# Spectral filter rows: 14 of 32 GpSimd gathers replaced by plain strided copies on the sync queue

## Chip, cores and metric

One core of one Trainium2 chip. The metric is the device time of one launch in microseconds (us), the median over executions. "Before" is the tuned kernel, "after" the changed one.

## The reference, cut to what matters

```python
x = A_x                                          # [1, 2048, 640] bf16
xn = _layernorm(x)
X = rfft2(xn, axes=(-2, -1))                     # 2048 x 321 complex
s = irfft2(X * (A_w_r + 1j * A_w_i))             # filter: 2048 x 321, two bf16 arrays
g = silu((gelu(xn @ B_w_gate) * (xn @ B_w_up)) @ B_w_down)
return x + s * g
```

A spectral branch (a two-dimensional transform, a filter, the inverse) and a feed-forward branch (three large matrix products) are computed side by side. The change touches only how the rows of the filter reach on-chip memory.

## The kernel before: the parts that matter

The transform along the sequence is done as matrix products. Its frequencies come in eight groups G of 128 rows. For each group the filter is needed twice: at the frequencies k (`pm = 0`, "positive") and at the mirrored ones 2048 - k (`pm = 1`), real and imaginary part each. A row is 321 values, 642 bytes. All four pieces were fetched by indirect gathers on GpSimd (POOL), with the row numbers in a table `LANE`:

```python
WF = [persist.tile([P, 2, 2, LP], BF16, name=f"WF{i}") for i in range(3)]   # three filter buffers
# ...
def gather(G):
    sw = Slot("W")

    def go(e):
        sw.tile = WF[G % 3]
        if 0 < G < 3:      # a 1x1 copy that reads BU: holds groups 1 and 2 back until BU has landed
            nc.gpsimd.tensor_copy(out=gate, in_=sB.tile[0:1, 8 * G - 8, 0:1])
        for pm in range(2):
            for ri, wsrc in enumerate((A_w_r, A_w_i)):
                nc.gpsimd.indirect_dma_start(
                    out=sw.tile[:, pm, ri, 0:L], out_offset=None, in_=wsrc,
                    in_offset=bass.IndirectOffsetOnAxis(ap=LANE[:, 2 * G + pm:2 * G + pm + 1], axis=0))
    W_in[G] = add(go, "POOL", (4200, 4200), (3, G), ...)      # estimated cost in ns, rank
# ... the only two readers, on VectorE:
def m1(e):    # L651
    nc.vector.tensor_tensor(out=sM.tile, in0=sw.tile, in1=sV.tile, op=ALU.mult)
def m3(e):    # L659, after it WF[G % 3] may be filled for group G + 3
    nc.vector.tensor_tensor(out=sN.tile, in0=sw.tile, in1=sV.tile[:, :, ::-1, :], op=ALU.mult)
```

The kernel does not issue its work in the order of the text. Each piece is a task with an estimated cost and a rank, and a small planner in Python lays the tasks out in time; what each engine executes, and in which order, follows from that plan. An engine works its list in order. Semaphore waits are added from the data that an instruction reads and writes.

Names in the profiles: `WF` filter rows, `BU` the regrouped transform input in on-chip memory, `zt`, `Z`, `ma`, `mc` pieces of the spectral branch on VectorE (DVE) and ScalarE (ACT), `pg`, `pu` feed-forward products in PSUM, `ge`, `uT` what ACT and DVE make of them, `sp` PSUM of the spectral branch.

Of the kernel before, what the change touches and what calls it, by code (L numbers as in the profile page):

```python
# [16 lines left out]
P = 128  # L17
S = 2048
D = 640
L = 321  # L20
# [113 lines left out]
class Plan:  # L134
# [11 lines left out]
    def add(self, emit, eng, cost, rank, after=(), new=(), use=(), size=0, slow=1.0, hold=0):  # L146
        engs = eng if isinstance(eng, dict) else {eng: cost}
        t = Task(emit=emit, engs=engs, rank=rank, after=list(after), new=list(new), size=size, slow=slow, hold=hold, seq=len(self.tasks))
        for s in (*new, *use):
            s.users.append(t)  # L150
        self.tasks.append(t)
        return t
# [70 lines left out]
def c_dve(n, rate=2, psum=False, extra=0):  # L223
    d = ((120 if psum else 58) + n / rate) / 0.96 + extra
    return d + 10, d + 130
# [3 lines left out]
def kernel(  # L229
# [11 lines left out]
    nc = tc.nc  # L241
# [22 lines left out]
    gate = consts.tile([1, 1], BF16)  # L264
# [9 lines left out]
    WF = [persist.tile([P, 2, 2, LP], BF16, name=f"WF{i}") for i in range(3)]  # L274
# [12 lines left out]
    add = plan.add  # L287
# [15 lines left out]
    def dma(out, in_, rank, size, after=(), new=(), use=(), slow=1.0, eng=None):  # L303
        return add(lambda e: nc.sync.dma_start(out=out() if callable(out) else out, in_=in_() if callable(in_) else in_),  # L304
                   "SP", (430, 430), rank, after=after, new=new, use=use, size=size, slow=slow)
# [54 lines left out]
    def keep_warm(n, after, src=None):  # L360
        def go(e):
            if heat.tile is None:
                place(heat, (2, 512))
            for k in range(n):
                nc.tensor.matmul(heat.tile[:, k % 2, :], lhsT=idle.tile[:, 0:P], rhs=idle.tile if src is None else X[:, src, 0:512],
                                 start=True, stop=True, skip_group_check=True)
        return add(go, "PE", (n * 430, n * 430), (0, -9), after=after, new=[] if heat.users else [heat], use=[idle, sX] + ([heat] if heat.users else []))
    t = add(blank, "DVE", (330, 400), (0, -9), new=[idle])
    t = keep_warm(6, [t])
# [3 lines left out]
    t = keep_warm(4, [t, x_in[0]], 0)  # L373
# [19 lines left out]
    turned, stored, xn_of = {}, {}, {}  # L393

    def stats(n1, engs):
        x = X[:, n1, :]
        mean, var, rstd = MVA[:, n1, 0:1], MVA[:, n1, 1:2], RSTD[:, n1, :]
        junk = Slot("th")

        eng = engs[0]  # L400
        after = [x_in[n1]] + ([aps[3]] if n1 > 3 else [])

        def moments(e):
            for g in range(2):
                nc.vector.bn_stats(out=STAT[:, n1, 6 * g:6 * g + 6], in_=x[:, 320 * g:320 * g + 320])  # L405
            nc.vector.bn_aggr(out=MVA[:, n1, :], in_=STAT[:, n1, :].rearrange("p (g s) -> p g s", g=2))
            nc.vector.tensor_scalar_add(out=var, in0=var, scalar1=1e-5)  # L407

        def total(e):
            nc.scalar.activation(out=place(junk, (D,)), in_=x, func=ACT.Copy, scale=-1.0 / D, accum_out=NM[:, n1, :])  # L410

        def square(e):
            nc.scalar.activation(out=junk.tile, in_=x, func=ACT.Square, scale=1.0, bias=NM[:, n1, :], accum_out=var)
        if eng == "DVE":
            t = add(moments, "DVE", (1200, 1340), (2, n1), after=after, use=[sX])
        else:
            t = add(total, "ACT", (870, 1000), (2, n1), after=after, new=[junk], use=[sX])
            t = add(square, "ACT", (930, 1100), (2, n1), after=[t], use=[junk, sX])

        def root(e):  # L420
            if eng == "ACT":
                nc.gpsimd.tensor_scalar(out=var, in0=var, scalar1=1.0 / D, scalar2=1e-5, op0=ALU.mult, op1=ALU.add)
            nc.gpsimd.tensor_tensor(out=rstd, in0=var, in1=mh, op=ALU.pow)  # L423
        n = 0 if eng == "DVE" else 1
        return add(root, "POOL", (300 * n + 600, 300 * n + 700), (1, n1), after=[t]), eng
# [84 lines left out]
    for n1 in range(NSLAB):  # L510
        if n1 % 2 == 0:
            xn_of[n1 // 2] = Slot("s1")
        r = stats(n1, (lead[n1] if n1 < 4 else ("ACT" if n1 % 2 else "DVE"),))
# [10 lines left out]
    sB = Slot("xb")  # L524
    B_in = {}
# [18 lines left out]
    W_in, W_slot = {}, {}  # L544

    def gather(G):
        sw = Slot("W")

        def go(e):
            sw.tile = WF[G % 3]  # L550
            if 0 < G < 3:
                nc.gpsimd.tensor_copy(out=gate, in_=sB.tile[0:1, 8 * G - 8, 0:1])
            for pm in range(2):
                for ri, wsrc in enumerate((A_w_r, A_w_i)):
                    nc.gpsimd.indirect_dma_start(  # L555
                        out=sw.tile[:, pm, ri, 0:L], out_offset=None, in_=wsrc,
                        in_offset=bass.IndirectOffsetOnAxis(ap=LANE[:, 2 * G + pm:2 * G + pm + 1], axis=0))
        W_in[G] = add(go, "POOL", (4200, 4200), (3, G), use=[sB] if 0 < G < 3 else [], after=[stored[7]] + ([W_in[G - 1], B_in[2 * G - 2]] if 0 < G < 3 else [W_in[G - 1]] if G else []), new=[sw],
                      size=328704, slow=1.3)
        W_slot[G] = sw  # L560
    for G in range(8):
        gather(G)
    for k in ("t2", "fm", "ft"):
# [7 lines left out]
    def spectral(G):  # L571
# [39 lines left out]
        for ri in range(2):  # L611
# [14 lines left out]
            def cp(e, ri=ri, pe=pe):  # L626
                if ri == 0:
# [4 lines left out]
                    after=[z_done, zt_done, tab_in["fm"], tab_in["ft"]] + firsts)  # L632
            firsts.append(a)
            es.append(add(cp, either(644, act=150), None, (1, 102 + 10 * G), after=[a] + es, use=[pe, sE]))
        sV = Slot("mb")
# [9 lines left out]
        rk = (1, 103 + 10 * G)  # L645
        t = add(v1, "DVE", (810 + (480 if G == 0 else 0), 900 + (480 if G == 0 else 0)), rk, after=es, new=[sV], use=[sE])
        sw, sM, sN, sY, sR = W_slot[G], Slot("mc"), Slot("mc"), Slot("Y"), Slot("R")
# [16 lines left out]
        def m5(e, h):  # L664
            if h == 0:
                place(sR, (2, 2, LP))
            R, Y = sR.tile, sY.tile[64 * h:64 * h + 64]
            Yf = Y.rearrange("p a b f -> p (a b) f")
            for ri in ((1, 0) if h else (0, 1)):
                o = R[64 * ri:64 * ri + 64, h]  # L670
                if ri:
                    nc.vector.tensor_tensor(out=o, in0=Yf[:, ::-3, :], in1=Yf[:, 1:3, :], op=ALU.subtract)
                else:
                    nc.vector.tensor_tensor(out=o, in0=Y[:, 0], in1=Y[:, 1], op=ALU.add)
            if G == 0 and h == 0:
                nc.vector.tensor_copy(out=R[0:1, 0], in_=Y[0:1, 0])
                nc.vector.tensor_scalar_mul(out=R[64:65, 0, 0, :], in0=Yf[0:1, 3, :], scalar1=-1.0)
                nc.vector.tensor_copy(out=R[64:65, 0, 1, :], in_=Yf[0:1, 2, :])
        t = add(m1, "DVE", c_dve(1288), rk, after=[t, W_in[G]], new=[sM], use=[sw, sV])
        t = add(m2, "DVE", c_dve(644), rk, after=[t], new=[sY], use=[sM])  # L680
        t = add(m3, "DVE", c_dve(1288), rk, after=[t], new=[sN], use=[sw, sV])
        t = add(m4, "DVE", c_dve(644), rk, after=[t], use=[sN, sY])
        sI, ius = Slot("IU"), []
        for h in range(2):
            ex = 750 if G == h == 0 else 0
            t = add(lambda e, h=h: m5(e, h), "DVE", (960 + ex, 1050 + ex), rk, after=[t], new=[] if h else [sR], use=[sY, sR] if h else [sY])
# [15 lines left out]
    for G in range(8):  # L702
        spectral(G)
# [212 lines left out]
```

## Time and profile before

| before | value | where |
|---|---|---|
| time, median of the first three executions | 206.83 us (206.66 to 206.9) | the times |
| span of the profiled execution | 209.8 us | the page |
| PE busy | 199.8 us, 95% | the page, part 1 |
| DVE busy / POOL busy | 161.2 / 55.6 us | the page, part 1 |
| gathers on POOL | 32, 33.2 us together | the page, part 5 |
| longest idle time of PE | 2.5 us, at 72.1 to 74.5 us | the waits of PE |

The page of before. In parts 1 and 5 the columns are busy time, share or mean, and idle time with what ended most of it; the row "POOL" with digits is busy tenths in 40 slices.

```profile
PE 199.8 (95%) x1385; PEld 119.9 (57%) x1385; DVE 161.2 (77%) x340; ACT 106.2 (51%) x185; POOL 55.6 (27%) x83
PE   7899899999999779999999999999999999999992
...
PE 77%; DMA 9%; DVE 6%; SPq 4%; ACT 2%; issue 1%; ACTq 0%; DVEq 0%
...
L555 POOL DMA_INDIRECT WF<-in_A_w_r_dram,LANE x16 | 16.5, 1034 | 25.3 <-DVE mc L659 22.5
L555 POOL DMA_INDIRECT WF<-in_A_w_i_dram,LANE x16 | 16.7, 1044 | 4.9 <-issue 4.9
```

PE is full except at the ends and in one place (the two sevens in the middle). The gathers wait for a free buffer (`mc L659`), and nothing in the chain is a gather. In the view of the tile WF the first reader, L651, has no idle time before it; the gathers themselves are the only ones that wait (us, times):

```profile
L651 DVE TENSOR_TENSOR mc<-WF,mb x8: 809/824/829, 80.9 to 128.2; 128x1288 bf16<-128x1288 bf16 x8
...
who waited for it (us, times):
  POOL WF L555: 22.5, 5
```

The longest waits of PE in before, longest in total first (us in total, times, longest):

```profile
PE sp L619 <- DVE zt L297: 2.5, 1, 2.5
PE sp L365 <- DVE uT L358: 1.2, 1, 1.2
```

The timeline of before around that wait (start, us, engine, line, what, and in brackets the idle time before it with what ended it):

```profile
69.30 0.61 PE L582 MATMUL sp<-T,BU 128*128 128x128 bf16 x8
...
69.44 0.95 POOL L555 DMA_INDIRECT WF<-in_A_w_r_dram,LANE  x1 [0.30 <-issue]
...
70.69 0.95 POOL L555 DMA_INDIRECT WF<-in_A_w_i_dram,LANE  x1 [0.31 <-issue]
70.83 1.24 PE L793 MATMUL pg<-xnT,Wg 128*128 128x512 bf16 x5
73.13 1.08 ACT L805 ACTIVATE ge<-pg 128x512 bf16<-128x512 f32 x2 [3.69 <-PE pg L793]
73.25 1.23 DVE L297 CAST zt<-sp 128x1024 bf16<-128x1024 f32 x1 [2.19 <-PE pg L793]
...
74.53 0.45 PE L619 MATMUL sp<-FT,zt 128*128 128x322 bf16 x2 [2.46 <-DVE zt L297]
```

The product `L582` that the cast `zt` reads was, by its own record, through at 69.91 us. DVE was free from 71.06 us on. Yet the cast began at 73.25, and what ended its wait was a signal of PE. ACT waited 3.69 us for PE in the same place.

### The profile page before, as it was taken

To read this page: it belongs to the slowest core of one execution; us is meant where nothing else is said; L and a number is where in the kernel's file an instruction comes from. 1 tells how busy PE (TensorE), PEld (TensorE's weight loads), DVE (VectorE), ACT (ScalarE), POOL (GpSimd) and SP (SyncE) were. 2 spreads that over 40 slices of the span, in tenths; PEclk is the share of its full clock that TensorE was granted. 3 is DMA by queue.
4 is the path that set the end of the run, shared out by engine and by line. 5 is a ranking of instruction groups with operands and counts; after the bars stand their busy time and mean duration, and the time that the engine had idled before them with its cause. 6 is when DMAs were issued, how large, how long until landed. Compare 5 with 4: busy or idle time off the path is not lost.

```text
span 209.8 us, 3765 instructions
## 1 busy us (share of the span) xinstructions
PE 199.8 (95%) x1385; PEld 119.9 (57%) x1385; DVE 161.2 (77%) x340; ACT 106.2 (51%) x185; POOL 55.6 (27%) x83
## 2 busy tenths in 40 slices
PE   7899899999999779999999999999999999999992
PEld 2574344575545356677765444457775656645771
DVE  3897989996324179999989999992366999994464
ACT  4685962444333147867766434322356758642221
POOL 3513422073027500725755810000000222221100
PEclk9999999999999999999999999999999999999999
DMA  6999999699589500113333251016900444542022
GB/s 196 308 318 323 363 285 254 107 285 168 175 279 351 164 3 0 44 41 108 107 97 112 60 160 62 5 62 177 387 3 0 125 128 125 166 130 82 30 67 63
DMA packets 30947, 31.07 MB, mean 148 GB/s; under 512 B 10417, under 2 KB 27457, under 8 KB 30929
## 3 DMA queue, kind: packets, MB, share of 16 engines
q1 hardware_dynamic: 27696, 24.32, 40.0%
q0 software_dynamic: 2368, 5.30, 9.8%
q10 hardware_dynamic: 864, 1.21, 1.6%
q8 instruction: 11, 0.18, 0.4%
q14 instruction: 8, 0.06, 0.1%
HBM read 20.99 MB, written 7.86 MB: 138 GB/s over the span
## 4 chain that ended last, share of the span: by engine, by line
PE 77%; DMA 9%; DVE 6%; SPq 4%; ACT 2%; issue 1%; ACTq 0%; DVEq 0%
PE pg L793 19%; PE pu L793 19%; PE pu L853 12%; PE pg L853 12%; DMA X<-in_A_x_dram 5%; SPq L304 4%; DMA D<-mc 3%; PE sp L692 2%; PE sp L619 2%; PE sp L623 2%; PE sp L724 2%; PE sp L737 2%; PE sp L734 2%; PE sp L599 2%; DVE uT L809 1%
## 5 line engine op out<-in xcount | busy, mean ns | idle before, releaser
L793 PE MATMUL pu<-xnT,Wu 128*128 128x512 bf16 (+1 forms) x270 | 60.7, 356 | 0.0
L793 PE MATMUL pg<-xnT,Wg 128*128 128x512 bf16 (+1 forms) x270 | 60.7, 356 | 0.0
L805 ACT ACTIVATE ge<-pg 128x512 bf16<-128x512 f32 x48 | 28.4, 596 | 42.0 <-PE pg L793 38.5
L853 PEld LDWEIGHTS <-uT 128*128 128x128 bf16 x396 | 37.7, 98 | 14.2
L809 DVE TENSOR_TENSOR uT<-pu,ge 128x512 bf16<-128x512 f32 x48 | 33.0, 688 | 12.7 <-PE pu L793 6.8
L793 PEld LDWEIGHTS <-Wg 128*128 128x128 bf16 x270 | 24.6, 98 | 23.4
L793 PEld LDWEIGHTS <-Wu 128*128 128x128 bf16 x270 | 24.4, 98 | 22.4
L853 PE MATMUL pg<-Wd,uT 128*128 128x320 bf16 (+2 forms) x204 | 31.7, 293 | 0.0
L853 PE MATMUL pu<-Wd,uT 128*128 128x320 bf16 (+1 forms) x192 | 31.0, 298 | 0.0
L818 POOL DMA_DIRECT2D xr<-in_A_x_dram x16 | 8.7, 547 | 70.5 <-DVE res L841 70.5
L297 ACT CAST ma<-sp 128x644 bf16<-128x644 f32 (+1 forms) x28 | 21.8, 794 | 9.2 <-PE sp L623 4.4
L555 POOL DMA_INDIRECT WF<-in_A_w_r_dram,LANE x16 | 16.5, 1034 | 25.3 <-DVE mc L659 22.5
L862 ACT ACTIVATE th<-pg 128x320 f32<-128x320 f32 (+2 forms) x17 | 7.3, 429 | 21.6 <-PE pg L853 18.2
L555 POOL DMA_INDIRECT WF<-in_A_w_i_dram,LANE x16 | 16.7, 1044 | 4.9 <-issue 4.9
L867 DVE SCALAR_TENSOR_TENSOR G<-th,pg 128x320 bf16<-128x320 f32 (+2 forms) x17 | 8.0, 471 | 11.4 <-ACT th L862 10.5
L423 POOL TENSOR_TENSOR RSTD<-MVA,mh 128x1 f32<-128x1 f32 x16 | 9.9, 618 | 22.2 <-DVE MVA L407 21.6
L867 DVE SCALAR_TENSOR_TENSOR G<-th,pu 128x320 bf16<-128x320 f32 (+1 forms) x16 | 7.7, 482 | 6.9 <-ACT th L862 6.9
L297 ACT CAST Vt<-sp 128x640 bf16<-128x640 f32 x13 | 8.8, 693 | 5.7 <-PE sp L724 5.7
L405 DVE BATCH_NORM_STATS2 STAT<-X 128x6 f32<-128x320 bf16 x18 | 7.9, 482 | 2.7 <-DMA X<-in_A_x_dram 2.7
L297 ACT CAST IU<-sp 128x640 bf16<-128x640 f32 x12 | 8.2, 692 | 3.4 <-PE sp L692 2.8
L862 ACT ACTIVATE th<-pu 128x320 f32<-128x320 f32 (+1 forms) x16 | 7.0, 440 | 5.3 <-PE pu L853 4.8
L619 PE MATMUL sp<-FT,zt 128*128 128x322 bf16 x32 | 7.0, 301 | 2.5 <-DVE zt L297 2.5
(80 smaller groups left out, 248.9 us busy)
## 6 DMA issues: line engine op xcount, KB each, us to landing
BU<-D SPq DMA_DIRECT2D x8, 640.0 KB
D<-mc SPq DMA_DIRECT2D x8, 320.0 KB
D<-IU SPq DMA_DIRECT2D x8, 320.0 KB
xr<-in_A_x_dram POOLq DMA_DIRECT2D x16, 160.0 KB
out_dram<-res SPq DMA_DIRECT2D x15, 160.0 KB
Wg<-in_B_w_gate_dram SPq DMA_DIRECT2D x6, 320.0 KB
Wu<-in_B_w_up_dram SPq DMA_DIRECT2D x6, 320.0 KB
Wd<-in_B_w_down_dram SPq DMA_DIRECT2D x2, 960.0 KB
```

Of the source, the lines that this page charges most:

```text
L297: return nc.scalar.copy(out=out, in_=in_) if e == "ACT" else nc.vector.tensor_copy(out=out, in_=in_)
L304: return add(lambda e: nc.sync.dma_start(out=out() if callable(out) else out, in_=in_() if callable(in_) else in_), "SP", (430, 430), rank ...
L423: nc.gpsimd.tensor_tensor(out=rstd, in0=var, in1=mh, op=ALU.pow)
L555: nc.gpsimd.indirect_dma_start(out=sw.tile[:, pm, ri, 0:L], out_offset=None, in_=wsrc, in_offset=bass.IndirectOffsetOnAxis(ap=LANE[:, 2 * ...
L619: nc.tensor.matmul(pt[:, bank, 0:LP], lhsT=tl, rhs=FT[:, ft, :], start=True, stop=False, skip_group_check=True)
L793: nc.tensor.matmul(ps.tile[:, lo:hi], lhsT=w[:, c, t * P:(t + 1) * P], rhs=xnT[:, c, grp * 512 + lo:grp * 512 + hi], start=(c == 0), stop= ...
L805: nc.scalar.activation(out=ge.tile, in_=pg.tile, func=ACT.Gelu_apprx_tanh)
L809: nc.vector.tensor_tensor(out=u.tile, in0=pu.tile, in1=ge.tile, op=ALU.mult)
L818: nc.gpsimd.dma_start(out=sx.tile, in_=xv[:, n1, :])
L853: nc.tensor.matmul(ps.tile[:, 0:hi - lo], lhsT=uT[grp, t].tile[:, j * P:(j + 1) * P], rhs=Wd[:, t, lo:hi], start=(t == 0), stop=(t == 11))
L862: nc.scalar.activation(out=th.tile[:, 0:hi - lo], in_=ps.tile[:, 0:hi - lo], func=ACT.Tanh, scale=0.5)
L867: nc.vector.scalar_tensor_tensor(out=G2.tile[:, lo:hi], in0=th.tile[:, 0:hi - lo], scalar=1.0, in1=ps.tile[:, 0:hi - lo], op0=ALU.add, op1 ...
```

## The change

Its intent: the positive rows k are regular (16 blocks of 4 neighbouring rows, 128 apart, for each half of the partitions), so no gather is needed for them. For groups 1 to 7 they are copied by four plain strided DMAs of 64 rows on the sync queue (SP), and POOL gathers only the mirrored rows: 18 gathers instead of 32, 28 copies more. Bytes and row length stay the same.

```diff
     def gather(G):
-        sw = Slot("W")
+        sw, got, pms = Slot("W"), [], (1,) if G else (0, 1)
# ... the gate copy moves into go_held; POOL's estimated cost is 2100 ns per pm
-            for pm in range(2):
+            for pm in pms:
                 for ri, wsrc in enumerate((A_w_r, A_w_i)):
                     nc.gpsimd.indirect_dma_start(...)
# ...
+        if G == 0:
+            return
+        for h in range(2):
+            for ri, wsrc in enumerate((A_w_r, A_w_i)):
+                k = 8 * G + 4 * h
+                got.append(dma(lambda h=h, ri=ri: WF[G % 3][64 * h:64 * h + 64, 0, ri, 0:L],
+                               wsrc.rearrange("(k r) f -> k r f", r=P)[:, k:k + 4, :], (0, 1, 100 + G), 41088,
+                               after=got[:1], use=[sw], slow=1.3))
# ... m1 waits for all of W_in[G]
```

More of the change, by code (lines that the diff above doesn't have):

```diff
@@ L546, in gather @@
     def gather(G):
-        sw = Slot("W")
+        sw, got, pms = Slot("W"), [], (1,) if G else (0, 1)
         def go(e):
             sw.tile = WF[G % 3]
-            if 0 < G < 3:
-                nc.gpsimd.tensor_copy(out=gate, in_=sB.tile[0:1, 8 * G - 8, 0:1])
-            for pm in range(2):
+            for pm in pms:
                 for ri, wsrc in enumerate((A_w_r, A_w_i)):
@@ L557, in go, with go_held @@
                         in_offset=bass.IndirectOffsetOnAxis(ap=LANE[:, 2 * G + pm:2 * G + pm + 1], axis=0))
-        W_in[G] = add(go, "POOL", (4200, 4200), (3, G), use=[sB] if 0 < G < 3 else [], after=[stored[7]] + ([W_in[G - 1], B_in[2 * G - 2]] if 0 < G < 3 else [W_in[G - 1]] if G else []), new=[sw],
-                      size=328704, slow=1.3)
-        W_slot[G] = sw
+        held = [B_in[2 * G - 2]] if 0 < G < 3 else []
+        def go_held(e):
+            if held:
+                nc.gpsimd.tensor_copy(out=gate, in_=sB.tile[0:1, 8 * G - 8, 0:1])
+            go(e)
+        cost = 2100 * len(pms)
+        got.append(add(go_held, "POOL", (cost, cost), (3, G), use=[sB] if held else [], after=[stored[7]] + W_in.get(G - 1, [])[:1] + held,
+                       new=[sw], size=164352 * len(pms), slow=1.3))
+        W_in[G], W_slot[G] = got, sw
+        if G == 0:
[6 more added lines that the diff above has]
+                               after=got[:1], use=[sw], slow=1.3))
     for G in range(8):
@@ L678, in m5 @@
                 nc.vector.tensor_copy(out=R[64:65, 0, 1, :], in_=Yf[0:1, 2, :])
-        t = add(m1, "DVE", c_dve(1288), rk, after=[t, W_in[G]], new=[sM], use=[sw, sV])
+        t = add(m1, "DVE", c_dve(1288), rk, after=[t] + W_in[G], new=[sM], use=[sw, sV])
         t = add(m2, "DVE", c_dve(644), rk, after=[t], new=[sY], use=[sM])
```

## The prediction

> **What bounds the kernel now.** The matrix engine. The page's busy table gives PE 199.8 of 209.8 us (95%); the windows view by 10 us gives PE 9.8 to 10.0 of 10 in every window from 80 to 200 us, at a granted clock of 1.00. PE is idle for 10 us in all: about 2 at the start, 4.3 in the last window, and a hole of 2.5 us at 72-74.5 us (waits: "PE sp L619 <- DVE zt"). The chain of waits is 77% PE and 9% DMA (x loads, D2 store), with no filter gather and no POOL in it.
>
> **The part that changes.** 32 gathers (L555, 1.03-1.04 us each, 33 us of POOL's 55.6 busy), four per group, about 1.3 us apart. Nothing waits for them: the tile view of WF shows L651, their first consumer, with no idle time before it in any of its eight runs; the only waits are POOL's own, for a buffer ("POOL WF <- DVE mc L659", 22.5 us) and for BU (12.1). Group 0's end at 49.4 for a multiply at 80.9, those of groups 1 and 2 at 71.6; refills run from 84.5, two groups ahead.
>
> **What the change does.** 14 gathers go (about 14.5 us; POOL busy to about 41). In their place the sync queue issues 28 copies of 64 rows of 642 B. At 0.33-0.45 us an issue (as the other stores on that queue) that is 9-12 us of SP within 57-118 us, where SP now waits up to 31.8 us at a stretch. Bytes and row length stay, so DMA load does. The Trainium skill ("DMA: Bandwidth & Descriptors", Issuing engines are not separate DMA queues) says that all issuers share the same 16 DMA engines and that spreading issues saves only sequencer time; here POOL has that time to spare. DVE gets some more semaphore waits (50 ns or less each at L651): an estimated 1-2 us in all, on an engine 77% busy.
>
> **On the critical path: directly nothing.** Three indirect routes remain.
> 1. The kernel orders its instructions by a plan from estimated costs; shorter POOL tasks and more SP tasks shift spectral against feed-forward work. PE's total stays, its holes may move: plus or minus 1 us.
> 2. The stretch 59-70 us is DMA-saturated (share 0.90-1.19 in 1 us windows) and the 2.5 us hole stands at its end, where ACT, DVE and PE all lag while gathers drain till 73. With half the gathers it may shrink by 0-1.5 us. This trace doesn't show that the gathers cause it.
> 3. SP is in order: a copy waiting for a free WF buffer may hold back a D3 store by about 1 us. Only the last store matters (140.8 us); the copies are done by about 120.
>
> **Prediction.** 206.4 us, 204.6 to 208.0 in 8 of 10. Faster by over 2% (under 202.7): 0.04; within 2%: 0.92; slower by over 2%: 0.04.
>
> **What would show it.** 18 gathers of about 1 us on POOL; 28 WF copies on SP; PE still 199-200 us busy; no wait for WF before L651; the chain still about 77% PE; PE full from 80 to 200 us; a hole of 0 to 3 us near 70-75 us.
>
> **What would make it wrong.** Slower: SP copies blocking a store or load that something waits for, or DVE stalling on late copies until PE runs out of fill work: PE holes after 76 us. Faster by over 2%: more than 4 us of PE's idle 10 would have to go, the middle hole and half of the ends, which the change doesn't touch.

## More of the kernel before

The runs of this study fell on two chips, numbered 8 and 14 in the records; for the first measurement of before and after no chip number is recorded. All runs are of one core.

## The result, and the profile after

| | median us | lowest to highest | executions |
|---|---|---|---|
| before | 206.87 | 206.66 to 207.61 | 4 |
| after | 207.06 | 206.92 to 207.19 | 4 |

The ratio of after to before is 1.0007 (95% interval 0.9987 to 1.0028): the same.

The page of after:

```profile
PE 198.5 (97%) x1385; PEld 120.1 (59%) x1385; DVE 161.0 (78%) x340; ACT 106.6 (52%) x185; POOL 41.8 (20%) x69
PE   7799999999999999999999999999999999999991
...
PE 90%; DMA 4%; SPq 1%; ACT 1%; DVE 1%; issue 0%; ACTq 0%
...
L553 POOL DMA_INDIRECT WF<-in_A_w_r_dram,LANE x9 | 9.8, 1084 | 33.9 <-DVE mc L672 32.9
L553 POOL DMA_INDIRECT WF<-in_A_w_i_dram,LANE x9 | 9.7, 1073 | 2.7 <-issue 2.7
```

18 gathers, POOL at 41.8 us, PE's two sevens in the middle gone. The new copies and their first reader in after (duration of the issue in ns, minimum, median, maximum):

```profile
L304 SPq DMA_DIRECT2D WF<-in_A_w_r_dram x14: 536/563/667, 58.2 to 110.2; - x14
L304 SPq DMA_DIRECT2D WF<-in_A_w_i_dram x14: 536/589/1839, 58.9 to 110.8; - x14
...
L664 DVE TENSOR_TENSOR mc<-WF,mb x8: 810/820/828, 76.8 to 123.2; 128x1288 bf16<-128x1288 bf16 x8
```

The same place in the timeline of after; lines of all engines, in order of time:

```profile
67.83 0.61 PE L595 MATMUL sp<-T,BU 128*128 128x128 bf16 x8
...
69.09 1.21 DVE L297 CAST zt<-sp 128x1024 bf16<-128x1024 f32 x1
69.35 1.24 PE L806 MATMUL pg<-xnT,Wg 128*128 128x512 bf16 x5
...
70.43 0.44 PE L632 MATMUL sp<-FT,zt 128*128 128x322 bf16 x2
70.63 0.60 ACT L818 ACTIVATE ge<-pg 128x512 bf16<-128x512 f32 x1 [1.69 <-PE pg L806]
```

The product that the cast reads ended by its record at 68.44 (67.83 + 0.61), the cast began at 69.09, straight behind the instruction before it, and PE took its result up without a wait. The hole is gone and the profiled span is 4.5 us shorter, 205.3 against 209.8. But the times do not differ. Both can be true only if the profiled execution of before was not like the timed ones. Two facts from the builds narrow the question: the lists of instructions of PE, of DVE and of ACT are the same in both kernels, in the same order; only POOL's and SP's lists differ. So the plan did not move any compute.

The trace also records when each semaphore was raised. PE posts one signal per group of matmuls; put side by side with the recorded ends of the groups, in order, they give this for the execution of before just shown (us; from 51 to 66.2 and again from 75 to 90, signal and recorded end agree within 0.1):

```
recorded end   signal    late
66.23          66.24     0.0
67.31          68.82     1.5     the gathers of groups 1 and 2 run on POOL from 61.8
68.39          70.28     1.9     to 71.6 us, eight in a row; their last DMA packet
69.47          73.10     3.6     starts at 72.98 us
69.69          73.16     3.5
69.91          73.22     3.3     <- the product that the cast zt waits for
70.99          73.29     2.3
72.07          73.36     1.3
```

Five signals arrive within 0.26 us. One group of five matmuls takes 1.08 us, so this work was not done in that time: it had been done, and the signals were held back. Over whole traces some signals are not recorded, so there I matched signals and groups such that the lateness is least, and count those over 0.4 us late; these counts and sizes are lower bounds. In before's trace at least 14 signals of PE are late (three near 50 us, behind group 0's four gathers, those of the table, and five from 97 to 106 us, among the refills), in after's none. No signal of ACT, DVE or POOL is late in either.

### The profile page after: what moved, and what is told of

It reads as the page before. It is cut to its first block, busy times and chain, and to the rows that moved or that the text cites. A ratio compares the mean times of both kernels' runs of the same rounds, so it can differ in the third digit from the quotient of the medians.

```text
span 205.3 us, 3793 instructions
## 1 busy us (share of the span) xinstructions
PE 198.5 (97%) x1385; PEld 120.1 (59%) x1385; DVE 161.0 (78%) x340; ACT 106.6 (52%) x185; POOL 41.8 (20%) x69
## 4 chain that ended last, share of the span: by engine, by line
PE 90%; DMA 4%; SPq 1%; ACT 1%; DVE 1%; issue 0%; ACTq 0%
PE pg L806 24%; PE pu L806 24%; PE pg L866 13%; PE pu L866 12%; DMA X<-in_A_x_dram 4%; PE sp L636 2%; PE sp L737 2%; PE sp L750 2%; PE sp L632 2%; PE sp L705 2%; PE sp L747 2%; PE sp L612 2%; PE sp L498 2%; SPq L304 1%; PE sp L595 0%; ACT th L410 0%
## 5 line engine op out<-in xcount | busy, mean ns | idle before, releaser
L553 POOL DMA_INDIRECT WF<-in_A_w_r_dram,LANE x9 | 9.8, 1084 | 33.9 <-DVE mc L672 32.9
L553 POOL DMA_INDIRECT WF<-in_A_w_i_dram,LANE x9 | 9.7, 1073 | 2.7 <-issue 2.7
L297 ACT CAST mc<-sp 128x640 bf16<-128x640 f32 x11 | 7.2, 692 | 3.3 <-PE sp L499 3.3
```

The source lines that it names most:

```text
L297: return nc.scalar.copy(out=out, in_=in_) if e == "ACT" else nc.vector.tensor_copy(out=out, in_=in_)
L553: nc.gpsimd.indirect_dma_start(out=sw.tile[:, pm, ri, 0:L], out_offset=None, in_=wsrc, in_offset=bass.IndirectOffsetOnAxis(ap=LANE[:, 2 * ...
```

## Experiments

Two theories at the start. **Off the path**: the filter loads are hidden and PE sets the time, so nothing about the loads matters; before's page shows an odd execution. **Two effects cancel**: the gathers cause the hole, and the copies cost as much elsewhere.

### First series, chip 8

**Before, unchanged, and after, unchanged.**

> The kernel before, unchanged, with its own profile: is the 2.5 us PE hole at 72-74.5 us of the first profile, and its span of 209.8 us (3 us longer than the median time), usual or a matter of that one execution? Theory 'off the path' (filter loads hidden, PE sets the time): ratio 1.000 +- 0.003 and a profile span of about 205 us with PE idle about 6-8 us and no hole over 1 us at 70-76 us. Rival 'two effects cancel' (the gathers cause the hole, and the new copies cost as much elsewhere): the hole of 2-3 us is there again and the span stays over 208 us.

> The change again, five rounds, to put a narrow interval on its effect. Off the path: 0.998 to 1.003 of before. Rival: the same total, but a profile in which PE has holes over 1 us after 76 us that before lacks.

Measured on chip 8: before 213.94 us (its repeats as the kernel to compare with: 214.14 median of 11), after 207.91 us. The ratio of after to before is 0.9728 (0.9699 to 0.9757), a gain of 2.7%. Neither theory had allowed for this: on this chip the change is clear of noise, and it is before that is slow, by 7 us against the first measurement.

The longest waits of PE in before on chip 8, the same hole, and a second one at about 103 us:

```profile
PE sp L619 <- DVE zt L297: 2.7, 1, 2.7
...
PE sp L619 <- ACT IU L297: 0.9, 1, 0.9
```

Three windows of 10 us of before and then of after on chip 8 (busy us and instructions of each engine, then PE's granted clock, DMA share, GB/s):

```profile
60.00:70.00 10.00, 9.95 (x65) 5.25 (x64) 3.30 (x4) 3.25 (x5) 6.71 (x9) 1.00 1.04 357
70.00:80.00 10.00, 7.25 (x60) 4.54 (x59) 5.91 (x10) 3.60 (x6) 1.28 (x2) 1.00 0.10 21
80.00:90.00 10.00, 9.95 (x77) 6.06 (x75) 9.57 (x21) 8.24 (x11) 4.00 (x4) 1.00 0.10 25
```

```profile
60.00:70.00 10.00, 9.95 (x65) 5.26 (x64) 3.99 (x6) 3.29 (x5) 4.22 (x6) 1.00 1.05 328
70.00:80.00 10.00, 9.89 (x77) 6.24 (x78) 8.58 (x16) 5.92 (x8) 0.00 (x0) 1.00 0.09 29
80.00:90.00 10.00, 9.95 (x79) 6.42 (x80) 9.53 (x19) 7.36 (x11) 2.17 (x3) 1.00 0.15 34
```

PE loses 2.6 us (9.89 less 7.25) in the middle window of before against after. Before has at least 16 late signals, after 2, both at group 0's four gathers. The spread of before has a second part: over its six executions here, spans of 210.2, 210.8, 212.1, 212.3, 212.8 and 213.3 us go with mean granted clocks of 0.998, 0.997, 0.991, 0.989, 0.988 and 0.984. So in most executions with the larger loss PE's clock is lower for a while (one of the 11 repeats does not fit: 211.9 us at 1.000); runs below show where.

**Before without the refills.** An early return leaves out the gathers of groups 3 to 7 (relative error 0.044). Its output is wrong, which doesn't matter for the time.

```diff
         if 0 < G < 3: ...
+            if G > 2:
+                return
             for pm in range(2):
```

> Before with the 20 gathers of groups 3 to 7 left out, so the multiplies reuse stale filter rows (wrong result on purpose); the instruction orders of PE, DVE and ACT are unchanged. Off the path: 206.9 us, ratio 0.997 to 1.002, although 21 us of POOL work and 1.6 MB of DMA are gone. Rival: gathers cost something by contention, so 1 to 4 us faster (ratio 0.98 to 0.995).

Measured: 212.78 us, ratio 0.9913 (0.9869 to 0.9958). With 20 of 32 gathers gone the kernel is 0.9% faster, so the gathers, or the 1.6 MB that they fetch, do cost something without anyone waiting for their data (clear of 1, not of 2%). The hole at the gathers of groups 1 and 2, which this kernel keeps, is still there, and the granted clock in the window from 70 to 80 us is 0.83. The longest wait of PE:

```profile
PE sp L621 <- DVE zt L297: 3.1, 1, 3.1
```

**Before with two more gathers per group** into a tile that nobody reads.

```diff
+    WX = persist.tile([P, 2, 2, LP], BF16, name="WX")
# ... in go, behind the four gathers
+            for ri, wsrc in enumerate((A_w_r, A_w_i)):
+                nc.gpsimd.indirect_dma_start(out=WX[:, 1, ri, 0:L], ..., in_offset=... LANE[:, 2 * G + 1 ...])
```

> Before with two more gathers per group into a tile that nobody reads (48 instead of 32), behind the real ones. POOL per group goes from 5 to about 7.8 us against a group spacing of about 7 us. Off the path: ratio 0.998 to 1.004, L651 still without a wait for WF. Rival: 1 to 3 us slower by contention alone.

Measured: 231.99 us, ratio 1.0851 (1.0804 to 1.0898). Off the path expected at most 1.004, the rival at most 3 us. Both fell. The longest wait of PE in this run, and its windows:

```profile
PE sp L625 <- DVE zt L298: 8.3, 1, 8.3
```

```profile
60.00:70.00 10.00, 9.95 (x65) 5.28 (x65) 3.30 (x4) 2.96 (x5) 6.89 (x9) 1.00 1.05 353
70.00:80.00 10.00, 1.70 (x9) 0.62 (x8) 2.02 (x3) 1.20 (x2) 4.91 (x6) 0.85 0.22 55
80.00:90.00 10.00, 9.78 (x67) 6.25 (x69) 6.74 (x14) 4.72 (x6) 0.00 (x0) 0.81 0.01 2
```

From 70 to 80 us PE, DVE and ACT all but stand still while POOL gathers, with DMA nearly idle (share 0.22): bandwidth is not what is short. The wait of PE for `zt` is 8.3 us here. The granted clock falls to 0.81 to 0.85, so after the hole PE also runs slower for some us: that is a second part of the loss. At least 28 signals of PE are late.

From this came a third theory, **bursts of gathers**: three or more gathers in a row on POOL hold back PE's signals; the change helps because it turns runs of four into runs of two, and the run of eight at 60 to 72 us into two pairs with a pause. Its rival now, **filter latency**: the rows simply arrive sooner.

### Second series, chip 8

Before took 213.79 us (212.12 to 215.32, 7 executions) in this series.

**After with two unread gathers more** per group 1 to 7 (the edit as above, `if G`), so that four stand in a row again.

> New theory 'bursts of gathers': a run of three or more gathers in a row on POOL makes the matrix engine's completion signals arrive late (in the first kernel's trace up to 3.4 us late at 69-72 us), and ACT, DVE and then PE wait for them. This kernel is the change with two more gathers per group (1 to 7) into a tile that nobody reads, so that each group issues four in a row again, while the sync copies stay. Bursts: the gain is lost, time like before on the same chip (ratio 0.99 to 1.01), PE hole of 2 us or more at 66-76 us, late PE signals in the trace. Rival 'filter latency' (the change wins because rows are there sooner): still like the change, ratio about 0.973 where before takes 214 us.

Measured: 214.81 us, ratio 1.0053 (0.9965 to 1.0141). The whole gain is gone, though the copies and the early rows are still there; filter latency falls. 18 late signals, up to 3.7 us. The expected hole of over 2 us did not come in one piece: PE's waits are shorter and spread, and the granted clock falls to 0.83 here too. Three of its waits, and the window from 70 to 80 us:

```profile
PE pg L812 <- ACT ge L824: 1.6, 2, 1.4
PE pu L812 <- issue: 1.2, 1, 1.2
PE sp L711 <- ACT ma L298: 0.9, 1, 0.9
...
70.00:80.00 10.00, 8.17 (x46) 4.37 (x47) 5.30 (x8) 3.46 (x5) 0.72 (x1) 0.83 0.19 62
```

**The change for groups 1 and 2 alone, and for groups 3 to 7 alone** (edits of after).

```diff
-        sw, got, pms = Slot("W"), [], (1,) if G else (0, 1)
+        sw, got, pms = Slot("W"), [], (1,) if 0 < G < 3 else (0, 1)      # the other run: if G > 2
# ...
-        if G == 0:
+        if not (0 < G < 3):
             return
```

> The change for groups 1 and 2 alone (their eight gathers in a row at 60-72 us become four). Bursts: most of the gain, because the 2.5 us hole and the late signals at 68-73 us go: ratio 0.975 to 0.985 where before takes 214 us; the late signals of the later bursts of four stay. Filter latency: no gain, since groups 1 and 2 have their rows 10 us early.

> The change for groups 3 to 7 alone. Bursts: the hole of 2.5 us at 70-75 us stays, the late signals after 84 us go: ratio 0.990 to 0.998, near the 0.991 of the run that left those gathers out altogether. Filter latency: the whole gain, 0.973.

Measured: groups 1 and 2 alone 210.18 us, ratio 0.9806 (0.9740 to 0.9873); groups 3 to 7 alone 212.66 us, ratio 0.9945 (0.9885 to 1.0004, so not by itself clear of 1). The first is clear of 1 but not of 2%. Both are inside what bursts expected. The two gains, 1.9% and 0.6%, add to 2.5%, against 2.7% for the whole change on this chip in the first series. Most of it is the one run of eight gathers. At least 12 signals are still late in each of the two kernels; what a late signal costs depends on whether an engine is waiting for it. The wait of PE for `zt` in the second of these runs, with the first hole still in place, and its window:

```profile
PE sp L632 <- DVE zt L297: 2.9, 1, 2.9
```

```profile
70.00:80.00 10.00, 6.88 (x40) 4.12 (x40) 4.94 (x7) 2.85 (x4) 0.95 (x1) 0.83 0.07 19
```

Here too the granted clock drops behind the hole, to 0.83: the first two matmuls after it take 0.72 us together, against 0.45 in the first trace of before, where the clock held.

**Before, all 32 gathers, with a pause after every pair**: five POOL instructions on a 128x1 tile, about 1.3 us.

```diff
# ... in go, after the two gathers of each pm
+                for _ in range(5):
+                    nc.gpsimd.tensor_scalar(out=nap, in0=nap, scalar1=1.0, scalar2=0.0, op0=ALU.mult, op1=ALU.add)
```

> The kernel before with all 32 gathers, but with about 1.3 us of small POOL arithmetic after every pair, so never more than two in a row; POOL is busier than before and rows arrive later. Bursts: most of the gain of the change without its copies, ratio 0.973 to 0.985 where before takes 214 us, late PE signals gone. Rival 'number of gathers' or 'POOL busy': no gain or slower, 1.00 to 1.02.

Measured: 210.39 us, ratio 0.9828 (0.9772 to 0.9883). Nothing is removed, POOL is busier than ever (80.4 us), and 1.7% is gained (clear of 1, not of 2%). One late signal (0.5 us) is left of the 16. What it lacks against the change is a new wait that the pauses cause: rows now come too late for their reader.

```profile
who waited for it (us, times):
  POOL WF L557: 4.0, 2
  DVE mc L655: 3.9, 2
```

The last line is the first multiply waiting 3.9 us for WF, which no other run shows. PE's longest wait comes from there too, for `R`, which is made from that product; the hole at `zt` is gone:

```profile
PE sp L696 <- DVE R L676: 2.0, 2, 1.2
```

So on chip 8 it is neither the number of gathers nor POOL's busy time that costs, but gathers back to back.

### Third series: another chip

This series fell on chip 14, where before takes 206.76 us (206.46 to 207.63, 11 executions).

**After once more.**

> The change once more, beside the others on the same chip: 207.5 to 208.5 us and ratio 0.970 to 0.976 if it is the chip of the first two series; if it is another chip on which before takes about 207 us, ratio 0.998 to 1.003.

Measured: 206.93 us, ratio 1.0010 (0.9988 to 1.0032), the second of the two cases. The first measurement's picture is back: on this chip before has nothing to lose. All its 11 spans lie between 204.7 and 205.8 us. No trace of before on chip 14 was kept, so that its signals are in time there is inferred from the spans.

**The positive rows by plain copies on POOL's own queue.**

```diff
-            for pm in range(2):
+            for h in range(2 if G else 0):
+                for ri, wsrc in enumerate((A_w_r, A_w_i)):
+                    k = 8 * G + 4 * h
+                    nc.gpsimd.dma_start(out=WF[G % 3][64 * h:64 * h + 64, 0, ri, 0:L],
+                                        in_=wsrc.rearrange("(k r) f -> k r f", r=P)[:, k:k + 4, :])
+            for pm in ((1,) if G else (0, 1)):
```

> The filter rows of positive frequencies by the change's plain strided copies, but issued on POOL's queue where the gathers stood (per group 1 to 7: four plain copies of 64 rows, then two gathers, all in a row). Tells an indirect gather from any DMA that POOL issues. If only gathers in a row delay PE's signals: at most four gathers stand between copies, mostly two, so the gain of the change is kept, ratio 0.970 to 0.985 where before takes 214 us. If any run of POOL-issued DMAs does it: no gain, 0.99 to 1.02, late PE signals at 62-74 us.

Measured: 206.97 us, ratio 1.0012 (0.9984 to 1.0040), no late signal. This was meant to tell gathers from any DMA that POOL issues; on a chip that shows no loss it can't. Inconclusive for its question. It does show that on this chip, where no late signal was seen, it makes no difference which of the two queues issues the copies.

**After with two unread gathers of only 32 rows** per group (`WX[0:32, ...]`, `LANE[0:32, ...]`).

> As the run that added two unread gathers per group to the change and lost its gain (214.8 us), but each added gather fetches 32 rows, not 128. If the number of gather instructions in a row counts: the gain is lost again, over 212 us. If the amount of descriptors or bytes counts: most of the gain is kept, 208 to 210 us.

Measured: 207.45 us, ratio 1.0026 (0.9998 to 1.0054), no late signal. Its runs of gathers are again four and more in a row, so on chip 14 such runs do no harm at this size. Inconclusive for its question, since the wide version was not run on chip 14.

**After with a pause inside group 0**, a try at beating both.

> A try at beating both: the change with a pause of about 1.3 to 2.3 us of POOL arithmetic between the two pairs of group 0's four gathers, the only run of four that is left. Bursts: the 0.4 to 0.7 us of late PE signals at 48 us goes; PE has nothing waiting there, so 0 to 0.5 us faster than the change (207.4 to 208.0 where the change takes 207.9).

Measured: 207.81 us (206.71 to 208.63), ratio 1.0032 (1.0004 to 1.0060), against 1.0010 for after in the same series. No gain; there was nothing left to win here. No version beat after on chip 8 or before on chip 14.

## Why the prediction was right or wrong, point by point

- **The time**: 206.4 us, 204.6 to 208.0, same. Measured 207.06 us, and the same within 0.3%. Right, and right again on chip 14. In part this is luck: on chip 8 the same two kernels differ by 2.7%, an outcome to which the prediction gave 0.04, and nothing in it chose between the two cases.
- **"What bounds the kernel now: the matrix engine"**. Right, in its stretch from 80 to 200 us and in the total: PE's busy time is 197.2 to 198.5 us in all traces of after. The estimate that nothing over about 4 us could be had was made from this.
- **"On the critical path: directly nothing"**. Right. No trace of before or after shows a wait for WF before its first reader.
- **"Nothing waits for them"**, read as "they cost nothing". Wrong on chip 8. There the gathers hold back PE's signals; leaving the refills out gains 0.9%, two more per group lose 8.5%, pausing between pairs gains 1.7%. The step that failed is the one from "no one waits for their data" to "no one waits because of them".
- **Route 1, the plan moves compute, plus or minus 1 us**. It did not: PE's, DVE's and ACT's lists are identical.
- **Route 2, the hole "may shrink by 0-1.5 us"**. The right place and a wrong size. Where the hole exists, it went altogether: 2.7 us of waiting for `zt`, 0.9 us in the second one, and 6.0 us of median time on chip 8 (213.94 less 207.91). The two waits make 3.6 us of it; a lower clock is one part of the rest (0.984 to 0.998 in before's six executions, 0.995 to 1.000 in after's), and what remains is not accounted for piece by piece. Where it does not exist, 0. The prediction also said that the trace did not show the gathers as its cause; the signals in the same trace would have shown PE's part in it.
- **Route 3, SP holding back a store**: nothing of the kind is visible; the last D3 store (the copies `D<-IU` on SP) is issued by 136.3 us in after and by 141.1 in before.
- **SP's issue cost**: 0.33 to 0.45 us an issue was assumed, 9 to 12 us in all. Measured medians are 0.563 and 0.589 us, and with the long ones the 28 take 18.2 us. Off the path, so harmless. DVE's extra waits at the first multiply, 1 to 2 us by the prediction, come to some 0.3 us: 24 semaphore instructions instead of 18, at most 50 ns each.
- **The chain "still about 77% PE"**: it reads 90% in after, and again 90% on chip 8. But after's own trace from chip 14, with no late signal, has the chain below, so the share does not tell whether there is a hole; a part of the difference lies in which wait the chain follows in the first 40 us (in before it reaches PE at 39 us, after 7 us of the store `D<-mc` among others; in after it is on PE from 14 us on).

```profile
PE 78%; DMA 8%; DVE 5%; SPq 4%; issue 1%; ACT 1%; ACTq 0%; DVEq 0%
```
- **What was overlooked**: the page of before was that of an execution about 3 us longer than the timed ones. It was used to describe 206.8 us all the same.

The Trainium skill bears on three of these points. Its page "Perfetto Trace Analysis", Tensor Engine Instruction, says that the end of a matmul is estimated from its size and is a model, not a measurement. No run here measures the end itself; where nothing is held back the model is close to the signal (66.23 and 66.24 us), and in the hole it is far from it (69.91 and 73.22 us). "PE busy 95%" could therefore not show the fault. The page "DMA: Bandwidth & Descriptors", Issuing engines are not separate DMA queues, named in the prediction, says that spreading issues saves only sequencer time. On chip 14 the runs agree (ratios 1.001 both for copies on SP and on POOL). On chip 8 the change saved 6 us, but it also turned gathers into plain copies, and pauses on POOL's own queue gained 1.7%; so this is not shown to be against the page, only that sequencer time is not all that an issue can cost. And "SBUF — State Buffer", Who interferes with whom, says "PE and ACT never wait on anyone", which is about memory ports; no run here shows a port at fault, but PE's signals were held back by 4 us and more while POOL gathered.

**What stays open.** Why chip 8 and not chip 14. What holds the signals: descriptor writing, the completion signals of the gathers, or something else; the two runs meant to tell were spent on a chip without the effect. Whether any DMA issued by POOL does it, or gathers alone. And whether tracing has a part in it: the traces from chip 8 miss records of DMA completions (after has 2,029 of them there and 2,384 on chip 14), and no execution without records is at hand to compare. "Chip" is itself only a name for the two cases: there is one chip of each kind, and chip 14 was used in one later series alone.

The missing records say two things more. In the one complete trace (after on chip 14) there are 16 of them for each of 149 DMAs. By that count the four traces of chip 14 have 97.9% or more of theirs, and the eight of chip 8 have 66 to 86%: 78% for before, 85% for after, 86% for before with pauses, and 68% and 66% for the two runs with unread gathers, which also have the most late signals. So on chip 8 lost records and late signals go together, and recording stays a rival as a part of the cause. And the first trace of before has 1,692 of 2,160, or 78%, like before on chip 8, while the first trace of after has 2,372 of 2,384. So the two pages compared at the start were probably not taken under the same conditions, and the hole in one and not in the other must not be put down to the change alone; the experiments on chip 8 carry that. Whether before's fast executions of the first measurement ran where its profile was taken is not recorded.

## What to carry to other kernels

A load that nobody waits for can still cost time through what its issuing does to others, as on chip 8 here; test it by doubling it, halving it and spacing it out, not by looking for a wait. When an engine waits for a PE whose records say it was done, look at when the semaphore was raised, not at when the matmul ended. And compare the span of the profiled execution with the timed ones before reading the page, and the two kernels on more than one chip before calling them the same.

## What the Trainium skill lacked or had wrong

- "Perfetto Trace Analysis", Tensor Engine Instruction: it says that PE's end is estimated, and does not say how far the signal may come after it. Here at least 9 to 28 signals in a trace were 0.4 to over 4 us late on chip 8 in the kernels that fetch more than group 0 in runs of four or more gathers, and those held back together came 0.04 to 0.07 us apart at 50 and 73 us in before.
- "SBUF — State Buffer", Who interferes with whom ("PE and ACT never wait on anyone"): not wrong of ports as far as these runs go, but easily read too widely. With six gathers per group PE was busy 1.7 of 10 us from 70 to 80 us, and the kernel 8.5% slower.
- "DMA: Bandwidth & Descriptors", Issuing engines are not separate DMA queues: not wrong as far as these runs go (copies on SP and on POOL differ by nothing on chip 14, 1.0010 and 1.0012), but the section has no word on gathers holding up other engines' signals: turning 14 of 32 into plain copies on SP saved 2.7% on chip 8.
- "GPSIMD Engine Reference", Performance pitfalls for Q7 kernels: no word on gathers back to back. A pause of about 1.3 us after each pair gained 1.7% with all 32 gathers kept.
- No page has it that a kernel's time can differ between chips (or between the series run on them) by this much: before took 213.94 us on chip 8 and 206.76 us on chip 14, after 207.91 and 206.93.
